# Ten accumulating DMA issues moved behind GpSimd's small operations, and one difference moved to the split that uses it

## The chip, the cores and the metric

The kernel runs on one core of a Trainium2 chip. Five engines work from queues of their own, each strictly in its program's order: TensorE (PE in the profile; its weight loads are PEld), VectorE (DVE), ScalarE (ACT), GpSimd (POOL) and SyncE (SP, which here only issues DMAs). They meet through semaphores alone. The metric is the device time of one execution in microseconds, the median of several runs.

## The reference

A transformer block on x of 2048 tokens by 448 channels, all in float32, with six modulation vectors from a small product of silu(c):

```python
h = layernorm(x) * (1 + ca) + sa
x = x + ga * A(h)          # linear attention, 16 heads of 28
h = layernorm(x) * (1 + cb) + sb
x = x + gb * B(h)          # token-mixing MLP
# B: h' = layernorm(h); u = gelu(h'^T w1 + b1); y = u w2 + b2, transposed back
```

A computes q, k, v, applies phi(t) = t + 1 or exp(t), sums phi(k)^T v over the tokens, divides phi(q) times that sum by phi(q) times the sum of phi(k), and multiplies by wo. B mixes tokens: its first product contracts 2048 tokens into 1792 features for every channel, its second one goes back to 2048. Note that there are two norms in a row before B: the block's own, with its modulation, and the one inside B.

## The kernel before, in words

Tokens go in 16 tiles of 128 (NT), features in 14 blocks of 128 (NF). Every large product is made from float32 operands that are split into a high and a low part: high is a rounded copy made on ScalarE, low is the difference, and three matmuls (high by high, high by low, low by high) give the sum. The low part is made in one of two ways. `split` (line 81) lets VectorE subtract. For ten pieces of w1 (`PIECE_DMA`, pieces 8 to 17) `split_to` (line 309) does without VectorE: ScalarE writes high (line 316) and then minus high into the low tile (line 317), and a DMA that GpSimd issues adds the full value onto it (line 318, `accum_op` add).

The order of all work is written out by hand; the order in which the program's lines run is the order on each engine's queue. Tiles come from pools of equal slots, and a slot's next owner waits until the last reader of the old one is done.

**First stage around the change: the loop at line 891**, laps i = 0 to 20. A lap holds several tokens tiles at different depths, so that each engine finds work:

- TensorE: four transposes of tile i (lines 779 and 780, written to `tq`), eleven matmuls of the output product of tile i - 1 (L804), in the first laps a projection of q, and from lap 5 on twelve matmuls of B's first product with token tile i - 5 (`step`, lines 854 to 856, `up`). From lap 17 on twelve more, of the second group of features. Without a projection that is 27 instructions a lap.
- ScalarE: the copies of the transposes (`pth`, lines 784 and 785), the second norm's output `y` (L845, needs `nb` and `rt`) and its high part `h2h` (L848), the two sums of squares `sqa` and `sqb` (L330), then the two halves of a w1 piece (`ph`, `pl`, lines 316 and 317).
- VectorE: residual, products, both steps of the first norm (lines 823 and 827), the reciprocal of `den` (L764), the scaled `pn` that the next lap's transposes read (L768), the low part `h2l` (L851). In laps 13 to 16 one step of the last modulation vector each (`mod_part`, lines 235 and 237).
- GpSimd: `nb` = mean by reciprocal root (L844), `nm` = minus mean (L818), `den` plus a small number (L761), `ny` = minus mean (L832), and at the lap's end the variance `vw` (L837) and the reciprocal roots `rt` of both norms (L839). `rt` of one lap is read by `nb`, `y` and the first norm of the next.

`split_to` is called at the lap's end (line 959), so the DMA issue of a piece stands on GpSimd behind `rt` and ahead of the next lap's `nb`. Piece k is made in lap k - 2; pieces 0 to 15 are used in lap k + 5, pieces 16 and 17 in laps 17 and 18.

**Second stage: B's second product** (from line 1193 on). It is done for pairs of token tiles q = 0 to 7, each with seven products m = 0 to 6 of sums and differences of four quadrants of w2 (a11, a12, a21, a22; Strassen's scheme in Winograd's form): s1 = a21 + a22, s2 = s1 - a11, s3 = a22 - s2, s4 = a12 - s2. The first sum is made by a DMA that adds a22 onto a21 in place (line 1024). The others are made by `sub` (line 1026) on VectorE, two instructions each (pieces of 512 and 384 columns, L1030), called from `split7` (line 1040) behind the split of the product whose row in `PRODS` (line 1035) names them: s2 behind m = 1, s3 behind m = 2, s4 behind m = 3. The splits run ahead of the products in the order `cuts` (line 1126): (q, m) = (0,0), (0,1), (0,3), (1,0), (1,1), (0,2), (1,3) and so on. The first five of them, thus s2 of the second pair too, are called in the last lap of the first product (`PRE2`, line 35), ahead of the gelu, the product with the modulation (L988) and the operand sums of the last two feature blocks (`finish_u`, line 982; `ub`, `ta`, `tb`, `ut`), which run as jobs at the start of the second product.

Of the kernel before, what the change touches and what calls it, by code (L numbers as in the profile page):

```python
# [11 lines left out]
ALU = mybir.AluOpType  # L12
# [38 lines left out]
def block_kernel(ctx: ExitStack, tc: tile.TileContext, x, xt, wqkv, wo, w1, b1, w2, b2, c, wmod, wfirst, out):  # L51
    nc = tc.nc
# [25 lines left out]
    def bank(name):  # L78
        return psum.tile([P, 512], F32, name=name, tag="bank")

    def split(full, hi, lo):
        nc.scalar.activation(hi, full, AF.Copy)  # L82
        nc.vector.tensor_sub(lo, full, hi.bitcast(F32))  # L83
# [51 lines left out]
    def load_mod(j):  # L135
        for k in range(4):
            wm[j, k] = (tslot if j == 5 else slot)(f"wm{j}_{k}", parts=G)
            nc.sync.dma_start(wm[j, k], wmod[k * G:(k + 1) * G, j * D:(j + 1) * D])
# [55 lines left out]
    def mod_out(j, ps):  # L194
        mods[j] = cst.tile([P, D], F32, name=f"mod{j}")
        nc.scalar.activation(mods[j], ps[:, :D], AF.Copy, bias=1.0 if j == 4 else 0.0)
# [35 lines left out]
    def mod_part(j, k):  # L232
        if k == 0:
            macc[j] = (tslot if j == 5 else slot)(f"acc{j}", parts=G)
            nc.vector.tensor_scalar_mul(macc[j], wm[j, 0], sc[:G, 4:5])
        else:
            nc.vector.scalar_tensor_tensor(macc[j], wm[j, k], sc[:G, 4 + k:5 + k], macc[j], op0=ALU.mult, op1=ALU.add)


    def mod_split(j):  # L240
        acc = macc.pop(j)
        macc[j] = (moving(slot, f"mh{j}", parts=G), moving(slot, f"ml{j}", parts=G))
        split(acc, *macc[j])

    def mod_sum2(j):
        ps = bank(f"modp{j}")
        hi, lo = macc.pop(j)
        nc.tensor.matmul(ps[:, :D], ones_r[:G, :], hi, start=True, stop=False)
        nc.tensor.matmul(ps[:, :D], ones_r[:G, :], lo, start=False, stop=True)
        return ps  # L250
# [49 lines left out]
    def load_to(i):  # L300
        while done["load"] < min(i, len(pieces)):
# [4 lines left out]
                              w1[t * P:(t + m) * P, f0 * P:(f0 + n) * P].rearrange("(t p) f -> p t f", p=P))  # L306
            done["load"] += 1

    def split_to(i):
        while done["split"] < min(i, len(pieces)):  # L310
            k = done["split"]
            new = tslot if k in TOKP else slot
            hi, lo = new(f"ph{k}", dt=F32R, w=512), new(f"pl{k}", dt=F32R, w=512)
            if k in PIECE_DMA:
                full = raws.pop(k)
                nc.scalar.activation(hi, full, AF.Copy)
                nc.scalar.activation(lo, hi.bitcast(F32), AF.Copy, scale=-1.0)
                nc.gpsimd.dma_start(lo, full, accum_op=ALU.add)  # L318
            else:
                split(raws.pop(k), hi, lo)  # L320
            parts[k] = (hi, lo)
            done["split"] += 1
# [5 lines left out]
    def b_square(src, nm, acc, name):  # L328
        dst = junk if name[0] == "s" else slot(f"sq{name}")
        nc.scalar.activation(dst, src, AF.Square, bias=nm, accum_out=acc)  # L330
# [127 lines left out]
    def a_q(t):  # L458
        project(t, 0, "qp")
        qps[t] = close(t, 0)  # L460
        del heads[t]

    def a_exp_q(keep=0):
        for t in sorted(qps)[:len(qps) - keep]:
            q_exp(qps.pop(t), t)
# [309 lines left out]
    def b_transpose(t):  # L775
        pn = pns.pop(t)
        tps[t] = bank(f"tq{t}")
        for ch in range(3):
            nc.tensor.transpose(tps[t][:, ch * P:(ch + 1) * P], pn[:, ch * P:(ch + 1) * P], ident)
        nc.tensor.transpose(tps[t][:64, 384:], pn[:, 384:D], ident)  # L780

    def b_high(t):
        phs[t] = (slot(f"pth{t}", 512, F32R), slot(f"ptl{t}", 384, F32R))
        nc.scalar.activation(phs[t][0][:, :384], tps[t][:, :384], AF.Copy)
        nc.scalar.activation(phs[t][0][:64, 384:], tps[t][:64, 384:], AF.Copy)
# [9 lines left out]
    def b_out(t):  # L795
        ph, pl = phs.pop(t)
        opb[t] = bank(f"op{t}")
        todo = []
        for ch in range(3):
            s = slice(ch * P, (ch + 1) * P)  # L800
            todo += [(ph[:, s], Wph[ch]), (ph[:, s], Wpl[ch]), (pl[:, s], Wph[ch])]
        todo += [(ph[:, 384:], Wph[3]), (ph[:, 384:], Wpl[3])]
        for n, (a, b) in enumerate(todo):
            nc.tensor.matmul(opb[t][:, :D], a, b, start=(n == 0), stop=(n == len(todo) - 1))  # L804

    def b_sums(i):
        if i not in vss:
            vss[i] = small.tile([P, 2], F32, name=f"vs{i}", tag="vs")
        return vss[i]
# [20 lines left out]
    def b_mean2(t, i):  # L830
        nm2s[t] = small.tile([P, 1], F32, name=f"ny{t}", tag="ny")
        nc.gpsimd.tensor_scalar_mul(nm2s[t], sums.pop(t), -1.0 / D)  # L832
        b_square(ys[t], nm2s[t], b_sums(i)[:, 1:2], f"b{t}")
# [24 lines left out]
    def step(f0, t, accs, mh, ml):  # L858
        k, at = place[f0, t]
        hi, lo = parts[k]  # L860
        for i, ps in enumerate(accs):
            acc3(ps, hi, lo, slice(at + i * P, at + (i + 1) * P), mh, ml, t == 0, t == NT - 1)
        if place.get((f0, t + 1), (0, 0))[0] != k:
            del parts[k]
# [26 lines left out]
    for i in range(NT + LAG):  # L891
        if i == NT - 4:
            load_mod(5)
        if NT - 3 <= i <= NT:
            mod_part(5, i - NT + 3)
        if i == NT:
            mod_split(5)
        if i < NT:
            b_transpose(i)
        if 0 <= i - 1 < NT:  # L900
            b_out(i - 1)
        nq = min(len(late), QS.get(i, 1))
        for _ in range(nq):
            a_q(late.pop(0))
        t = i - LAG
        if t >= 0:
            if t == 0:
                accs = [bank(f"up{f}") for f in range(4)]
            if i > NT:
                if not early:  # L910
                    early = [bank(f"up{W1G[1][0] + f}") for f in range(W1G[1][1])]
                r = i - NT - 1
                step(W1G[1][0], r, early, H2h[r], H2l[r])
            step(0, t, accs, H2h[t], H2l[t])
        if i == NT:
            mp = mod_sum2(5)
            mod_out(5, mp)
        if i < NT:
            b_high(i)
        a_exp_q(nq)  # L920
        scale, res, norm1, norm2 = i + 1 < NT, 0 <= i - 2 < NT, 0 <= i - 3 < NT, 0 <= i - 4 < NT
        if res and i < NT + 1:
            b_res(i - 2)
        if scale:
            b_prod(i + 1)
        if norm2:
            b_norm2(i - 4, i)
        if res:
            b_mean1(i - 2, i)
        if norm1:  # L930
            b_norm1_a(i - 3)
        if scale:
            b_sum(i + 1)
        if norm1:
            b_norm1_b(i - 3, i)
        if scale:
            b_eps(i + 1)
        if i < NT:
            b_low(i)
        if norm1:  # L940
            b_mean2(i - 3, i)
        if scale:
            b_recip(i + 1)
        if i < NT:
            b_low_last(i)
        if scale:
            b_scale(i + 1)
        if i == NT:
            b_res(i - 1)
        if norm2:  # L950
            b_low2(i - 4)
        if i == 0:
            for ch in range(4):
                wp_split(ch)
        a_phi_q(nq)
        load_to(max(14 + (i + 1) // 2, 12 + max(0, i - 6) + max(0, i - 14)))
        if res or norm1:
            b_rstd(i, 0 if res else 1, 2 if norm1 else 1)
        split_to(8 + max(0, i - 5))
# [66 lines left out]
    def sub(q, out, a, b, op=ALU.subtract, into=None):  # L1026
        res = []
        for i, (r0, n) in enumerate(RS):
            w = raw2[q, into][i] if into else slot(f"{out}_{q}_{r0}", n * P)
            nc.vector.tensor_tensor(w, raw2[q, a][i], raw2[q, b][i], op=op)  # L1030
            res.append(w)
        raw2[q, out] = res


    PRODS = (("a11", "b11", 0, None), ("a12", "b21", 1, ("s2", "s1", "a11")),
             ("s2", "t2", 0, ("s3", "a22", "s2", ALU.subtract, "a11")),
             ("s1", "t1", 2, ("s4", "a12", "s2", ALU.subtract, "a12")), ("s3", "t3", 0, None),
             ("s4", "b22", 2, None), ("a22", "t4", 0, None))

    def split7(q, m):  # L1040
        a, _, _, add = PRODS[m]
        hilo[q, m] = []
        for w, (r0, nr) in zip(raw2[q, a], RS):
            h, l = slot(f"{a}h_{q}_{r0}", nr * P, F32R), slot(f"{a}l_{q}_{r0}", nr * P, F32R)
            split(w, h, l)
            hilo[q, m].append((h, l))
        if add:
            sub(q, *add)

    def mult7(q, m, r0, r1):  # L1050
# [215 lines left out]
```

## Time and profile before

| | |
|---|---|
| three runs | 445.61, 445.74, 446.75 us; median 445.74 |
| the profiled execution | 445.55 us, of which 443.7 are its span (first to last instruction) |
| granted TensorE clock, mean | 0.997 |
| busy: TensorE, VectorE, ScalarE, GpSimd | 434.0, 363.9, 278.8, 112.2 us |
| DMA | 65.94 MB, of it 14.78 by the queue that GpSimd feeds |

In the profile's rows a name like L318 is a line of the kernel; `out<-in` are the tiles written and read, with buffer numbers left out. A timeline row has start and length in us, engine, line, operation, tiles, shape and count, and in brackets the idle time of the engine before it with what ended it. A chain row has start, length, engine, tile and line. A wait row names the waiting line, the one waited for, the sum, how often and the longest. A matmul's drawn length contains its way through the array, and the next one starts before it ends.

### The profile page before, as it was taken

The numbers are of one execution on the slowest core, as the hardware profiler recorded it, in microseconds if no ns is written. First come the engines' busy times: TensorE is split into PE (matmuls) and PEld (weight loads), VectorE is DVE, ScalarE is ACT, GpSimd is POOL, SyncE is SP. The second block draws the span as 40 slices with busy tenths as digits, with TensorE's granted clock in tenths as the row PEclk, the third lists the DMA queues.
The fourth block names the chain that finished last, engine by engine and source line by source line (L and its number), as shares of the span: only waits on it lengthen the run. The fifth ranks groups of instructions, "written<-read, shape, count | busy, mean of one in ns | idle before, by whom it ended". The sixth has DMA issues, their size and how long they took to land.

```text
span 443.7 us, 7292 instructions
## 1 busy us (share of the span) xinstructions
PE 434.0 (98%) x2376; PEld 399.7 (90%) x2376; DVE 363.9 (82%) x821; ACT 278.8 (63%) x598; POOL 112.2 (25%) x201
## 2 busy tenths in 40 slices
PE   8999999999999999999999999999999999999996
PEld 7878899999899998889999999999989999999995
DVE  4989997699799999996569785829599998898893
ACT  4899877748667777776774263627285555645550
POOL 3227554200025455554300000010101331132010
PEclk9999999999999999999999999999999999999998
DMA  7997999555400035334516661578269977986332
GB/s 251 386 308 161 214 236 221 106 162 172 127 5 1 24 72 139 78 71 95 190 55 189 215 189 45 148 209 226 46 189 206 204 173 169 224 173 123 60 41 41
DMA packets 63797, 65.94 MB, mean 149 GB/s; under 512 B 4944, under 2 KB 55312, under 8 KB 63760
## 3 DMA queue, kind: packets, MB, share of 16 engines
q1 hardware_dynamic: 54688, 50.71, 38.0%
q0 software_dynamic: 9072, 14.78, 20.8%
q8 instruction: 18, 0.29, 0.3%
q14 instruction: 19, 0.16, 0.1%
HBM read 45.88 MB, written 7.34 MB: 120 GB/s over the span
## 4 chain that ended last, share of the span: by engine, by line
PE 79%; ACT 10%; DMA 3%; DVE 3%; POOL 2%; issue 2%; SPq 0%; POOLq 0%; ACTq 0%; DVEq 0%
PE y L1062 16%; PE y L1063 8%; PE cacc L524 8%; PE up L856 8%; PE up L855 8%; PE up L854 8%; PE qp L420 7%; PE kp L420 6%; PE op L804 3%; POOL pl L318 2%; ACT y L845 1%; ACT sqa L330 1%; DMA a<-in_B_w_dram 1%; DMA a<-a 1%; ACT sqb L330 1%
## 5 line engine op out<-in xcount | busy, mean ns | idle before, releaser
L855 PE MATMUL up<-h2l,ph 128*128 128x448 f32 x224 | 81.3, 363 | 0.0
L856 PE MATMUL up<-h2h,pl 128*128 128x448 f32 x224 | 81.2, 362 | 0.0
L854 PE MATMUL up<-h2h,ph 128*128 128x448 f32 x224 | 80.8, 361 | 0.0
L1024 POOL DMA_DIRECT2D a<-a x16 | 14.2, 958 | 143.0 <-DVE u L988 75.2
L855 PEld LDWEIGHTS up<-h2l,ph 128*128 128x128 f32 x224 | 42.0, 188 | 3.4 <-DVE h2l L851 0.3
L854 PEld LDWEIGHTS up<-h2h,ph 128*128 128x128 f32 x224 | 41.9, 187 | 3.0
L856 PEld LDWEIGHTS up<-h2h,pl 128*128 128x128 f32 x224 | 42.0, 188 | 2.3
L83 DVE TENSOR_TENSOR pl<-pr,ph 128x512 fp32r<-128x512 f32 x46 | 30.8, 686 | 4.1 <-ACT ph L82 3.3
L82 ACT ACTIVATE ph<-pr 128x512 fp32r<-128x512 f32 x46 | 27.6, 623 | 0.8 <-PE up L856 0.5
L1068 ACT ACTIVATE cc<-y 128x448 f32<-128x448 f32 x24 | 12.9, 542 | 21.3 <-PE y L1063 21.3
L1082 POOL DMA_DIRECT2D out_dram<-yt x15 | 13.5, 903 | 48.0 <-DVE yt L1073 37.4
L988 DVE TENSOR_TENSOR u<-u,mod 128x448 f32<-128x448 f32 x14 | 8.7, 621 | 19.8 <-ACT u L987 19.6
L524 PE MATMUL cacc<-pkh,xh 128*128 128x448 f32 x64 | 24.4, 382 | 0.3 <-ACT pkh L498 0.3
L804 PE MATMUL op<-wph,pth 128*128 128x448 f32 x64 | 24.5, 383 | 0.0
L987 ACT ACTIVATE u<-up,b1c 128x448 f32<-128x448 f32 x14 | 8.8, 625 | 24.1 <-PE up L856 23.5
L420 PE MATMUL kp<-wh,hh 128*128 128x448 f32 x64 | 23.2, 372 | 0.6 <-ACT wh L256 0.6
L524 PE MATMUL cacc<-pkl,xh 128*128 128x448 f32 x64 | 23.3, 364 | 0.2 <-DVE pkl L500 0.2
L420 PE MATMUL qp<-wh,hh 128*128 128x448 f32 x64 | 23.3, 364 | 0.0
L804 PE MATMUL op<-wpl,pth 128*128 128x448 f32 x64 | 23.1, 362 | 0.0
L845 ACT ACTIVATE y<-y,nb,rt 128x448 f32<-128x448 f32 x16 | 12.2, 761 | 12.7 <-POOL nb L844 12.7
L1062 PE MATMUL y<-ut,s1h 128*128 128x448 f32 x56 | 18.2, 376 | 0.6 <-DVE ut L83 0.6
L1030 DVE TENSOR_TENSOR a<-a,s 128x512 f32<-128x512 f32 (+1 forms) x32 | 18.4, 617 | 0.0
(236 smaller groups left out, 1368.0 us busy)
## 6 DMA issues: line engine op xcount, KB each, us to landing
pr<-in_B_w_dram SPq DMA_DIRECT2D x56, 256.0 KB, 3.2
a<-in_B_w_dram SPq DMA_DIRECT2D x32, 256.0 KB, 4.8
a<-in_B_w_dram SPq DMA_DIRECT2D x32, 192.0 KB, 4.6
xt<-in_xt_dram SPq DMA_DIRECT2D x16, 256.0 KB, 4.9
x<-in_A_x_dram SPq DMA_DIRECT2D x16, 224.0 KB, 4.9
out_dram<-x SPq DMA_DIRECT2D x15, 224.0 KB, 2.2
out_dram<-yt POOLq DMA_DIRECT2D x15, 224.0 KB, 6.3
wm<-in_B_wmod_dram SPq DMA_DIRECT2D x16, 196.0 KB, 5.1
```

The lines of the kernel that those rows point to most:

```text
L82: nc.scalar.activation(hi, full, AF.Copy)
L83: nc.vector.tensor_sub(lo, full, hi.bitcast(F32))
L420: nc.tensor.matmul(pps[t, j][:, :D], a[:, ch * P:(ch + 1) * P], w, start=first, stop=False)
L524: nc.tensor.matmul(cacc[ch][:, :D], a[:, s], b, start=(t == 0 and i == 0), stop=(t == NT - 1 and i == len(todo) - 1))
L804: nc.tensor.matmul(opb[t][:, :D], a, b, start=(n == 0), stop=(n == len(todo) - 1))
L845: nc.scalar.activation(ys[t], ys[t], AF.Identity, bias=nb, scale=rs)
L854: nc.tensor.matmul(ps[:, :D], hi[:, sl], mh, start=first, stop=False)
L855: nc.tensor.matmul(ps[:, :D], hi[:, sl], ml, start=False, stop=False)
L856: nc.tensor.matmul(ps[:, :D], lo[:, sl], mh, start=False, stop=last)
L1030: nc.vector.tensor_tensor(w, raw2[q, a][i], raw2[q, b][i], op=op)
L1062: nc.tensor.matmul(ps[:, :D], h[:, s], w, start=opens and r == 0, stop=False, skip_group_check=True)
L1063: nc.tensor.matmul(ps[:, :HD], l[:, s], wh, start=False, stop=closes and r == PAIRS - 1, skip_group_check=True)
```

## The change

The ten DMA issues are no longer written where the piece's low part is begun. `split_to` puts them in a list, and the loop at line 891 empties the list in its next lap, behind `b_mean2`, that is behind `nb`, `nm`, `den` and `ny` on GpSimd and ahead of `vw` and `rt`. The rows of pieces and everything ScalarE does for them stay where they were.

For the second pair alone, s2 is no longer made behind the split of m = 1 but behind the split of m = 3 (which splits s1), directly ahead of s4, which reads it. For all other pairs the order stays.

```diff
+    low_dma = []
+
+    def split_end():
+        while low_dma:
+            nc.gpsimd.dma_start(*low_dma.pop(0), accum_op=ALU.add)
+
     def split_to(i):
...
                 nc.scalar.activation(lo, hi.bitcast(F32), AF.Copy, scale=-1.0)
-                nc.gpsimd.dma_start(lo, full, accum_op=ALU.add)
+                low_dma.append((lo, full))
...
         if norm1:
             b_mean2(i - 3, i)
+        split_end()
         if scale:
             b_recip(i + 1)
...
             hilo[q, m].append((h, l))
-        if add:
+        if (q, m) == (1, 3):
+            sub(q, *PRODS[1][3])
+        if add and (q, m) != (1, 1):
             sub(q, *add)
```

## The prediction

> **What bounds the kernel now.** I began with the page: the busy shares, then the chain of waits by line.
>
> ```profile
> span 443.7 us, 7292 instructions
> PE 434.0 (98%) x2376; PEld 399.7 (90%) x2376; DVE 363.9 (82%) x821; ACT 278.8 (63%) x598; POOL 112.2 (25%) x201
> PE y L1062 16%; PE y L1063 8%; PE cacc L524 8%; PE up L856 8%; PE up L855 8%; PE up L854 8%; PE qp L420 7%; PE kp L420 6%; PE op L804 3%; POOL pl L318 2%; ACT y L845 1%; ACT sqa L330 1%; DMA a<-in_B_w_dram 1%; DMA a<-a 1%; ACT sqb L330 1%
> ```
>
> TensorE is busy 98% and carries most of the chain, so only time in which it stands still can be won. Yet a GpSimd DMA issue (L318), which computes nothing, holds 2% of the chain. So I read TensorE's own waits next (time, times, longest).
>
> ```profile
> PE tq L779 <- DVE pn L768: 1.8, 6, 0.5
> PE y L1062 <- DVE ut L83: 0.6, 1, 0.6
> ```
>
> The other five rows of that answer lie in the first 34 us. The change touches both of these: L779 opens each lap of the loop at line 891, L1062 is the first product pass. The loss is larger than these rows say, since a matmul is drawn 0.36 us long while the next starts after 0.20. The timeline of TensorE gives the starts of L779 in laps 7, 9 and 15 (start, length):
>
> ```profile
> 155.31 0.49 PE L779 MATMUL tq<-ident,pn 128*128 128x128 f32 x3
> ...
> 165.42 0.49 PE L779 MATMUL tq<-ident,pn 128*128 128x128 f32 x3
> ...
> 198.62 0.52 PE L779 MATMUL tq<-ident,pn 128*128 128x128 f32 x3 [0.54 <-DVE pn L768]
> ```
>
> Where TensorE doesn't wait, a lap takes (165.42 - 155.31) / 2 = 5.055 us; the next six take 33.20 together. At its own pace they would take 30.33, so 2.87 us are lost there. What sets the longer lap is in the chain in order of time:
>
> ```profile
> 163.46 0.77 ACT y L845
> 164.25 0.58 ACT h2h L848
> 164.83 0.65 ACT sqa L330 x2
> 165.48 0.65 ACT sqb L330 x2
> 166.13 0.53 ACT ph L316
> 166.69 0.63 ACT pl L317
> 167.32 0.39 ACT pth L784
> 167.72 0.94 POOL pl L318
> 168.66 0.24 POOL nb L844
> ```
>
> It is a closed ring, 168.92 - 163.46 = 5.46 us long: ScalarE's y to pl, then the issue of pl's DMA on GpSimd, then the small nb behind it in GpSimd's order, then the next y. The issue stands between pl and an nb that needs nothing of it.
>
> **The change, part by part.** It adds and removes no instruction; it moves ten DMA issues (pl 8 to 17) on GpSimd and two subtractions on VectorE.
>
> *The issues.* In the built order each goes from the head of GpSimd's lap (ahead of nb, nm, den, ny) to behind ny, ahead of vw and rt. No other queue is passed; behind the issue wait vw and rt alone, and rt is what the next nb and the next norm need. One lap of GpSimd:
>
> ```profile
> 162.25 0.94 POOL L318 DMA_DIRECT2D pl<-pr  x1 [0.27 <-ACT pth L784]
> ...
> 164.06 0.22 POOL L832 TENSOR_SCALAR ny<-sy 128x1 f32<-128x1 f32 x1
> 166.21 0.19 POOL L837 TENSOR_SCALAR vw<-vs 128x2 f32<-128x2 f32 x1 [1.93 <-ACT sqb L330]
> 166.49 0.97 POOL L839 TENSOR_TENSOR rt<-vw,mhalf 128x2 f32<-128x2 f32 x1
> ```
>
> GpSimd idles 1.93 us between ny and vw, and the issue takes 0.94: it goes into the hole. Two rings are left. ScalarE alone: from y at 163.46 to the end of pth at 167.71 is 4.25 us. Through rt: sqb lets vw start at 166.21, rt ends at 167.46, nb takes 0.24 behind a gap of 0.08, the next y would start at 167.81: 4.35. Both are under TensorE's 5.055, so TensorE takes the lap over, if VectorE lets it. VectorE's rows:
>
> ```profile
> 158.54 0.25 DVE L764 RECIPROCAL den<-den 128x16 f32<-128x16 f32 x1 [0.23 <-POOL den L761]
> ...
> 164.01 0.25 DVE L764 RECIPROCAL den<-den 128x16 f32<-128x16 f32 x1 [0.42 <-POOL den L761]
> ...
> 164.62 0.62 DVE L768 SCALAR_TENSOR_TENSOR pn<-pq,den 128x448 f32<-128x448 f32 x1
> ...
> 187.59 0.45 DVE L235 TENSOR_SCALAR acc<-wm,sc 112x448 f32<-112x448 f32 x1
> ...
> 193.15 0.68 DVE L237 SCALAR_TENSOR_TENSOR acc<-wm,sc,acc 112x448 f32<-112x448 f32 x1
> ```
>
> It waits for den, which stands behind the issue, nb and nm; with the issue gone den is 0.9 us earlier and the 0.42 falls away. VectorE's own lap is then 5.46 - 0.42 = 5.04, level with TensorE's. Is it ahead? The pn for the L779 of 165.42 ended at 165.24; without the two waits at 164.59. Six laps later, with the modulation rows of 0.45 and 0.68 in between and the 0.15 from pn's end to a waiting L779, it allows 164.59 + 30.24 + 1.13 + 0.15 = 196.11. TensorE's own pace gives 165.42 + 30.33 = 195.75. So the L779 of 198.62 comes between 195.75 and 196.15, and the gain is 2.5 to 2.9. I take 2.7: it is close between the engines, and the waits' true length is nearer 0.5 (VectorE's instructions overlap by some hundredths).
>
> The issue in its new place isn't in the trace. By the rows it costs from 0.92 (the shortest of its own) to 1.48 (the longest of its kind, L507):
>
> ```profile
> L318 POOL DMA_DIRECT2D pl<-pr x10: 920/937/965, 156.7 to 206.4; - x10
> ...
> DMA to landing us min/median/max: 3.3/3.4/6.3
> ...
> L507 POOL DMA_DIRECT2D pk<-pk x11: 877/1216/1484, 34.5 to 83.6; - x11
> ```
>
> If ScalarE starts sqb the moment ny is there, vw may start 0.85 behind ny's end (sqb 0.65, its readout and the step 0.2). An issue of length I, started 0.07 behind ny, then holds vw for I - 0.78: 0.16 us at 0.94, 0.70 at 1.48. The ring through rt grows from 4.35 to 4.51, or to 5.05, and still isn't the longest. So the move costs 0 at both ends of the rows. I take 0.94, its own median in the same loop.
>
> pl also lands later: the issue moves 164.28 + 0.07 - 162.25 = 2.1 us down the lap. Pieces 8 to 15 are used five or more laps later. The last, pl 17, is the tight one; its issue goes behind the ny of lap 16, and its first use is in the second row:
>
> ```profile
> 209.18 0.21 POOL L832 TENSOR_SCALAR ny<-sy 128x1 f32<-128x1 f32 x1 [0.79 <-DVE y L827]
> ...
> 214.15 0.36 PE L856 MATMUL up<-h2h,pl 128*128 128x448 f32 x1
> ```
>
> From 209.46 with 3.4 to the landing it is there at 212.9, 1.3 before its use; with the worst landing, 6.3, TensorE would stand 1.6 us, once. I take 0, by the median. The loads that reuse pr's buffers follow the landings, on SP's queue, but bring pieces 22 and on, which are used several steps behind piece 17.
>
> *The subtractions.* The second pair's s2 = s1 - a11 (L1030, two instructions) now stands on VectorE behind the split of s1 and ahead of s4 = a12 - s2. VectorE, TensorE and ScalarE before:
>
> ```profile
> 315.35 0.69 DVE L1030 TENSOR_TENSOR s<-a,a 128x512 f32<-128x512 f32 x1 [2.37 <-issue]
> 318.04 0.56 DVE L1030 TENSOR_TENSOR s<-a,a 128x384 f32<-128x384 f32 x1 [1.99 <-DMA a<-a]
> 318.51 0.62 DVE L988 TENSOR_TENSOR u<-u,mod 128x448 f32<-128x448 f32 x1
> ...
> 324.24 1.15 DVE L1030 TENSOR_TENSOR a<-a,s 128x512 f32<-128x512 f32 x2
> ...
> 325.14 0.27 PE L1063 MATMUL y<-ub,a12l 128*128 128x224 f32 x1
> 326.05 0.47 PE L1062 MATMUL y<-ut,s1h 128*128 128x448 f32 x1 [0.64 <-DVE ut L83]
> ...
> 330.86 0.38 PE L1062 MATMUL y<-ut,s3h 128*128 128x448 f32 x1
> 331.32 0.37 PE L1063 MATMUL y<-ut,s3l 128*128 128x224 f32 x1
> ...
> 314.15 0.64 ACT L987 ACTIVATE u<-up,b1c 128x448 f32<-128x448 f32 x1 [3.36 <-PE up L856]
> ```
>
> Both subtractions wait for an accumulating DMA, and everything VectorE still owes to the last pair of u is queued behind them. That u is ready at 314.79, but its product starts at 318.51: 3.7 us. From it hangs the ut for which TensorE waits at 326.05. Moved up by 3.7 it ends near 322.3, 2.9 before its use. In their new place the two cost what the x2 row of 324.24 costs, 1.1 us, ahead of s3l, which TensorE met at 331.32: -3.7 + 1.1 puts it 2.6 earlier, also in time. So TensorE's gaps close: 326.05 - 325.14 less the usual step 0.10 is 0.81; the slow step behind it 0.10; 331.32 - 330.86 less 0.21 is 0.25. Sum 1.16, the upper bound; the lower is 0, if the stall only changes its name. I take 1.16, as both margins are twice the gaps. Behind the first stage's gain all this comes 2.7 earlier; should the DMA not follow, it is now awaited by the s1 split, used at 328.7, with room.
>
> *The sum.* 2.7 + 1.16 = 3.86. The profiled execution took 445.55 (1.85 around its span): 441.7. The median shown, 445.74, lies 0.19 higher, which is inside this sum's error.
>
> **The rivals.** *VectorE binds the loop.* Its lap is as long as TensorE's, and GpSimd's issue now runs beside other VectorE work. At 5.2 a lap the L779 of 198.62 comes at 164.59 + 31.2 + 1.28 = 197.1, the gain is 1.5, and the time 445.55 - 2.7 = 442.9. For it: 5.04 against 5.055. Against: every VectorE length above already has GpSimd working beside it.
>
> *The second part pays nothing.* The 1.1 us in the new place, or ScalarE's splits behind it, make s3l or ut late again: 445.55 - 2.7 = 442.9. For it: s3l was late already, and the pair goes in ahead of it. Against: 4.4 us of VectorE's idle time (2.37 and 1.99) end.
>
> *Slower: the issue holds vw.* In the new place it runs beside VectorE's two-input operations (pn, h2l), and rt behind it closes the ring. If the issue had to sit out two such operations of 0.62, I = 2.2, vw is held 1.4, the lap is 5.75, and nine laps lose 9 x 0.29 = 2.6 against before; less 1.16 that is 447.0, and 452 with three. It decides above I = 1.9, where the lap is 5.46 again. Against: ten issues at 0.92 to 0.965 in a loop where VectorE is never idle for that long, and none of the eleven of L507 above 1.48. The Trainium skill ("SBUF — State Buffer", sections "SBUF: two separate sides" and "A bandwidth-pool intuition that's wrong (but worth ruling out)") speaks for this rival: GpSimd and VectorE share a port pair under an exclusive lock, and a GpSimd-issued DMA of about 620 ns takes about 3100 beside a VectorE copy. By its 3.1 the lap would be an estimated 6.67 and the time 455; the 0.94 of this loop disagrees.
>
> *It does nothing.* If the ring were closed by pth (the releaser that the profile names for the issue) and not by the issue, y would start no earlier: 444.4 with the second part's gain alone, 445.6 without it.
>
> **How the numbers follow.** Forecast 0.64, VectorE binds 0.12, second part nothing 0.12, slower 0.07, nothing 0.05. A difference under 0.3% (1.3 us) can't be told from none here; the first three lie beyond it: faster 0.88, same 0.05, slower 0.07. The range starts 0.7 under the forecast (the loop's full 2.9 is 0.2 of it, the scatter of the three runs below their median 0.13; the rest is left for what I have not seen) and ends at 443.6, which takes in both partial cases and half of one late landing: 441.0 to 443.6.
>
> **What would show it.** Right: L779 starts 5.05 apart through lap 15 and near 195.9 there; GpSimd's issue stands in the former idle time before vw, still about 0.94; ScalarE no longer waits for nb; L988 follows the last gelu at once; the waits for pn and ut are gone from TensorE's list. Wrong: issues over 1.5 us, vw waiting on the issue, L779 still 5.4 apart, a wait for pl near lap 18, or for s3l near 327.

## The result and the profile after

| | before | changed |
|---|---|---|
| median of six runs each, side by side | 445.94 us (445.61 to 447.34) | 442.79 us (441.48 to 443.62) |
| the profiled execution | 445.55 us | 442.58 us |
| its span | 443.7 us | 440.9 us |

The ratio is 0.992, 95% interval 0.9898 to 0.9942: a gain of 2.6 to 4.5 us. The forecast was 441.7.

The page of the changed kernel, its span, busy shares and the chain of waits by engine:

```profile
span 440.9 us, 7297 instructions
...
PE 432.9 (98%) x2376; PEld 400.8 (91%) x2376; DVE 363.2 (82%) x821; ACT 278.7 (63%) x598; POOL 119.2 (27%) x201
...
PE 94%; DVE 2%; ACT 1%; DMA 1%; SPq 0%; issue 0%; ACTq 0%
```

GpSimd's DMA issue and ScalarE's ring have left the chain; 94% of it is TensorE. TensorE's whole list of waits has five rows, all from the first 35 us:

```profile
PE warm L181 <- DVE roots L104: 1.1, 1, 1.1
PE rw L399 <- DVE rowst L391: 0.3, 1, 0.3
PE cacc L530 <- ACT pkh L504: 0.2, 1, 0.2
PE kp L426 <- ACT wh L256: 0.2, 1, 0.2
PE cacc L530 <- DVE pkl L506: 0.2, 1, 0.2
```

The waits for `pn` and `ut` are gone. In TensorE's timeline the first transpose of laps 6 and 15 (L785, L779 before) and the last matmul of the kernel:

```profile
150.32 0.49 PE L785 MATMUL tq<-ident,pn 128*128 128x128 f32 x3
...
195.80 0.38 PE L785 MATMUL tq<-ident,pn 128*128 128x128 f32 x2
...
434.93 0.26 PE L1072 MATMUL y<-ut,a22l 128*128 128x224 f32 x1
```

Nine laps take 195.80 - 150.32 = 45.48, that is 5.053 each. The same two ends before:

```profile
150.26 0.49 PE L779 MATMUL tq<-ident,pn 128*128 128x128 f32 x3
...
439.04 0.26 PE L1063 MATMUL y<-ut,a22l 128*128 128x224 f32 x1
```

From the first transpose of lap 6 to the last matmul it was 439.04 - 150.26 = 288.78 us, and is 434.93 - 150.32 = 284.61 now: 4.17 less. This stretch will be the yardstick below, because it leaves out how a run starts and how it ends. The span fell by 2.81 only. The missing 1.36 is 0.06 at the start and 1.30 at the end: from the last matmul to the end of the span it was 4.65 before and is 5.95 now. TensorE is done by then; two stores are in flight. The view of the plain store by line (tile 15's, two halves; the last to be issued is the max) gives their landing before, and then after:

```profile
DMA to landing us min/median/max: 1.7/2.1/2.5
```

```profile
DMA to landing us min/median/max: 1.7/2.7/3.6
```

The accumulating store of tile 14, issued by GpSimd 1.6 us ahead of that last half (434.49 in the changed kernel), landed after 4.95 us, against 3.63 before. So the loop gave all that was forecast and more, and the end of this one execution gave 1.3 back. Whether the change does that is the main thing to settle.

GpSimd in one lap of the changed kernel, and VectorE beside its `den`:

```profile
168.45 0.94 POOL L313 DMA_DIRECT2D pl<-pr  x1 [0.24 <-issue]
169.47 0.50 POOL L843 TENSOR_SCALAR vw<-vs 128x2 f32<-128x2 f32 x1
170.05 0.72 POOL L845 TENSOR_TENSOR rt<-vw,mhalf 128x2 f32<-128x2 f32 x1
170.85 0.20 POOL L850 TENSOR_TENSOR nb<-ny,rt 128x1 f32<-128x1 f32 x1
171.02 0.66 POOL L824 TENSOR_SCALAR nm<-sm 128x1 f32<-128x1 f32 x1
172.21 0.64 POOL L767 TENSOR_SCALAR den<-den 128x16 f32<-128x16 f32 x1 [0.52 <-DVE den L764]
```

```profile
171.51 0.61 DVE L764 TENSOR_REDUCE den<-pd 128x16 f32<-128x448 f32 x1
172.04 0.67 DVE L833 SCALAR_TENSOR_TENSOR y<-y,rt,mod 128x448 f32<-128x448 f32 x1
```

The issue fills the former hole and `nb` follows `rt` at once. It is GpSimd now that waits for VectorE's reduction (L764), not VectorE for `den`.

### The profile page after: what moved, and what is told of

It is laid out like the page before. It is cut to its first block, busy times and chain, and to the rows that moved or that the text cites. A ratio compares the mean times of both kernels' runs of the same rounds, so it can differ in the third digit from the quotient of the medians.

```text
span 440.9 us, 7297 instructions
## 1 busy us (share of the span) xinstructions
PE 432.9 (98%) x2376; PEld 400.8 (91%) x2376; DVE 363.2 (82%) x821; ACT 278.7 (63%) x598; POOL 119.2 (27%) x201
## 4 chain that ended last, share of the span: by engine, by line
PE 94%; DVE 2%; ACT 1%; DMA 1%; SPq 0%; issue 0%; ACTq 0%
PE y L1071 19%; PE up L860 10%; PE up L861 10%; PE up L862 10%; PE y L1072 9%; PE op L810 8%; PE cacc L530 8%; PE qp L426 7%; PE kp L426 6%; PE tq L785 1%; DMA xt<-in_xt_dram 1%; PE qp L433 1%; PE kvb L741 1%; PE rowb L283 1%; PE wp L877 1%; PE kp L433 1%
## 5 line engine op out<-in xcount | busy, mean ns | idle before, releaser
L995 DVE TENSOR_TENSOR u<-u,mod 128x448 f32<-128x448 f32 x14 | 8.7, 621 | 21.7 <-ACT u L994 21.5
L767 POOL TENSOR_SCALAR den<-den 128x16 f32<-128x16 f32 x16 | 8.8, 548 | 47.3 <-DVE den L764 47.3
L348 POOL TENSOR_TENSOR mv<-ve,roots 128x2 f32<-128x2 f32 (+1 forms) x13 | 12.8, 983 | 21.2 <-DVE ve L377 17.8
```

## The experiments

Every kernel was run beside the kernel before on its chip. "Stretch" is, as above, from the first L785 (or L779) at 150 to 151 us to the last matmul; "end" is from there to the end of the span; the last column is when the store issued last but one (tile 14's, on GpSimd unless it is plain) landed, counted from its issue.

| kernel | median us | ratio, 95% interval | stretch | end | landing |
|---|---|---|---|---|---|
| before | 445.94 | | 288.78 | 4.65 | 3.63 |
| changed | 442.79 | 0.992, 0.9898 to 0.9942 | 284.61 | 5.95 | 4.95 |
| e1 issues alone | 443.24 | 0.9927, 0.991 to 0.9944 | 285.99 | 4.82 | 3.79 |
| e2 subtraction alone | 445.65 | 0.9979, 0.9967 to 0.999 | 287.51 | 6.36 | 5.35 |
| e3 two issues each | 442.46 | 0.9904, 0.9889 to 0.9919 | 284.96 | 4.75 | 3.84 |
| e4 changed | 443.27 | 0.992, 0.9907 to 0.9933 | 284.61 | 6.38 | 5.38 |
| e5 issue behind nb | 443.38 | 0.9934, 0.992 to 0.9948 | 285.53 | 4.97 | 3.97 |
| e6 changed, plain store | 441.43 | 0.9888, 0.9873 to 0.9902 | 284.61 | 4.99 | plain |
| e7 four issues each | 453.23 | 1.0153, 1.0139 to 1.0168 | 295.16 | 6.05 | 5.17 |
| e8 changed, plain store | 441.08 | 0.9892, 0.9867 to 0.9916 | 284.61 | 4.69 | plain |
| e9 before, plain store | 445.46 | 0.9988, 0.9974 to 1.0003 | 288.28 | 5.08 | plain |
| e10 changed | 442.43 | 0.9922, 0.9897 to 0.9946 | 284.61 | 4.81 | 3.81 |

The medians of before were 446.73 beside e1 to e4, 446.12 beside e5 to e7, 445.79 beside e8 to e10.

### The two parts apart: e1, e2, e4

e1 is the changed kernel with s2 of the second pair back behind m = 1; e2 is the kernel before with only that subtraction moved; e4 is the changed kernel again. e1's edit against the changed kernel:

```diff
-        if (q, m) == (1, 3):
-            sub(q, *PRODS[1][3])
-        if add and (q, m) != (1, 1):
+        if add:
             sub(q, *add)
```

> The ten DMA issues stand behind ny as in the changed kernel; the second pair's s2 stays behind the split of m = 1. If the two parts are independent, TensorE's loop laps are 5.05 us through lap 15 and its waits for ut (0.8 us) and s3l (0.25) are back: the last matmul starts 2.8 to 2.9 us earlier than in the kernel before (at 436.2), and the time is 2.8 under it. If the second part was what paid, the last matmul moves by less than 1.5. Should the tail behind the last matmul (4.4 us in the kernel before, 5.7 in the changed one) be longer because of the moved issues, it is 5.7 here; if it varies by chance from execution to execution, it can be anything from 4.4 to 5.9.

> Only the second pair's s2 is moved; the issues stand ahead of nb as before. If the parts are independent: loop laps of 5.46 as before, no wait for ut or s3l, the last matmul 1.1 to 1.25 us earlier than in the kernel before, the time 1.1 to 1.2 under it. If the first part's gain is what makes the second one possible, the last matmul moves by less than 0.5. Tail by the theory that this part lengthens it: 5.7; by chance: 4.4 to 5.9.

> The changed kernel once more, for its tail. Its last matmul stood 4.1 us earlier than before, but its span was only 2.8 shorter. If the tail (last matmul to end of span) varies by chance with the landing of the last two stores, this execution has the last matmul at 434.9 again and a tail that can be anywhere between 4.4 and 5.9 us, and the times spread by about 2 us as before, with the fastest at 441.5. If the change makes the tail longer, it is 5.7 again.

TensorE's waits behind 150 us, first in e1, then in e2:

```profile
PE y L1069 <- DVE ut L83: 0.8, 1, 0.8
```

```profile
PE tq L779 <- DVE pn L768: 1.8, 6, 0.5
```

Each part takes away its own wait and leaves the other's. In the stretch the issues are worth 288.78 - 285.99 = 2.79 and the subtraction 1.27; together 4.06, of the 4.17. (e1's last matmul stands at 437.04 and not at the expected 436.2, because that execution reached lap 6 later, by 0.79.) The 0.11 between lies behind the loop. From the first transpose of lap 6 to that of lap 15 it is 48.36 before and 45.48 both in e1 and in the changed kernel: 2.88 less. Behind that, e1 waits 0.8 for `ut` where the kernel before waits 0.6. That the shorter loop makes this wait longer isn't shown, for in e9 below, whose loop is that of before, it is 0.2:

```profile
PE y L1062 <- DVE ut L83: 0.2, 1, 0.2
```

In all three VectorE waits for the DMA that adds a22 onto a21: 1.99 us before, 1.76 in e9, 2.10 in e1. So the second part takes away a wait whose length changes from one execution to the next. From lap 15 to the last matmul it is 240.42 before, 239.94 in e9 and 240.51 in e1, against 239.13 in the changed kernel and 239.15 in e2: this part is worth 0.8 to 1.4, and 1.27 is its worth against one execution of before.

In e4 the stretch is 284.61 again, to the hundredth, and so it is in e6, e8 and e10: what scattered between these executions of the changed kernel lay ahead of 150 us or behind the last matmul. For the kernel before the stretch did move, by 0.50 (e9). e4's times lay 0.84 apart, where some 2 was expected, and its end, like e2's, is longer than any that was expected.

### The place of the issue, and its length: e3, e5, e7

e3 doubles the suspected cost, e7 makes it four times as many; the bytes stay the same.

```diff
-                low_dma.append((lo, full))
+                low_dma.extend((lo[:, c:c + 256], full[:, c:c + 256]) for c in (0, 256))
```

In e7 the step is 128, four times. e5 calls `split_end()` behind `nb` already, ahead of `nm`, `den` and `ny`:

```diff
         if scale:
             b_prod(i + 1)
         if norm2:
             b_norm2(i - 4, i)
+        split_end()
...
-        split_end()
```

> The changed kernel, but each of the ten accumulating DMAs is issued as two of 256 columns, so that GpSimd spends 1.9 us on issues behind ny instead of 0.94. By the prediction's ring through rt the issue time costs nothing up to about 1.5 us and reaches the old lap at 1.9: with 1.9 the laps are 5.4 to 5.5 again, vw waits for the issue and not for sqb, ScalarE waits for nb again, the first part's gain of 2.9 us is gone, and the last matmul starts 1.1 to 1.5 us earlier than before. If GpSimd's place in the lap were free whatever stands there, the laps stay at 5.05 and the last matmul keeps its 4.1 us.

> The changed kernel, with each of the ten accumulating DMAs issued as four of 128 columns, some 3.7 us of issues in a lap. Theory (the issues share GpSimd's queue with vw, rt, nb, nm, den and ny; two of them, 1.87, filled it to 5.2 a lap, and TensorE's lead hid that): lap about 7.0, ScalarE waits 2 us or more for nb, TensorE waits for pn in each of laps 9 to 17, L785 of 195.80 comes 14 us or more later, time 455 to 460. Rival (the place behind ny is free whatever is put there, because nothing that sets the lap waits behind it): laps under 5.4, time under 446.

> The changed kernel, with the issue one place up: behind nb alone, still ahead of nm, den and ny. Theory (only nb closes the ring, nm and den have room): L785 stays 5.05 apart from lap 7 to 15, TensorE has no waits for pn, the gaps of TensorE's starts stay near 1.7 us in sum, last matmul within 0.3 of 434.9, time that of the changed kernel, 442.8 within 0.7. Rival (the den behind the issue was VectorE's wait and half of the gain): den comes 0.6 to 0.9 later than in the changed kernel, VectorE waits for it ahead of the reciprocal, its lap grows from 4.94 to 5.3 or more, L785 of 195.80 comes at 197.5 to 199, time 444 to 445.

e3, which should have been slower, lost nothing that its median shows, and 0.35 of the stretch. The timeline of one of its laps, and TensorE's first transpose of lap 15:

```profile
168.37 0.22 POOL L838 TENSOR_SCALAR ny<-sy 128x1 f32<-128x1 f32 x1
...
168.60 0.65 ACT L336 ACTIVATE sqa<-x,nm 128x448 f32<-128x448 f32 x1
...
168.84 1.87 POOL L313 DMA_DIRECT2D pl<-pr  x2 [0.24 <-ACT h2h L854]
...
169.26 0.66 ACT L336 ACTIVATE sqb<-y,ny 128x448 f32<-128x448 f32 x1
...
169.82 0.19 ACT L336 ACTIVATION_READ_ACCUMULATOR sqb<-y,ny 128x1 f32 x1
...
170.78 0.65 POOL L843 TENSOR_SCALAR vw<-vs 128x2 f32<-128x2 f32 x1
...
179.04 1.86 POOL L313 DMA_DIRECT2D pl<-pr  x2 [0.27 <-ACT h2h L854]
...
196.21 0.52 PE L785 MATMUL tq<-ident,pn 128*128 128x128 f32 x3 [0.17 <-DVE pn L774]
```

The issues do cost twice, 1.87. But `sqb` begins 0.67 behind the end of `ny`, since ScalarE is still at `sqa`; its readout ends at 170.01 and the issues at 170.71, so `vw` is held 0.70, not the 1.09 that the formula I - 0.78 gives. ScalarE now waits for `nb`, 5.3 us in eight laps, yet TensorE meets a late `pn` once, by 0.32 us (196.21 - 150.41 = 45.80 for nine laps, against 45.48). From 168.84 to 179.04 two laps of GpSimd take 10.20, that is 5.10 each, a little over TensorE's 5.055: the lead of the engines ahead of TensorE paid for the difference until lap 15.

e7 is where the cover ends. From GpSimd's timeline two laps' blocks of issues and three of the six operations between them, and ScalarE's only wait in 156 to 212 us:

```profile
179.53 3.63 POOL L313 DMA_DIRECT2D pl<-pr  x4
183.23 0.19 POOL L843 TENSOR_SCALAR vw<-vs 128x2 f32<-128x2 f32 x1
183.50 0.72 POOL L845 TENSOR_TENSOR rt<-vw,mhalf 128x2 f32<-128x2 f32 x1
...
185.12 0.27 POOL L767 TENSOR_SCALAR den<-den 128x16 f32<-128x16 f32 x1
...
185.65 3.64 POOL L313 DMA_DIRECT2D pl<-pr  x4
```

```profile
ACT y L851 <- POOL nb L850: 16.7, 8, 4.0
```

GpSimd works without a break from the one block to the next: 185.65 - 179.53 = 6.12 a lap, of which 3.63 are issues and 2.49 everything else. It has become the engine that sets the lap. The stretch is 10.55 longer than the changed kernel's and the time 453.23: far slower, as the theory said, but not the 455 to 460 that I expected, because I had added e3's longer `vw` and `rt` (0.65 and 1.04), which here take 0.19 and 0.72. One lap of 8.36 us has a hole of 2.25 on GpSimd ahead of its fourth issue that the profile puts down to nothing; its cause stays open. From 2.49 + I an estimate of the price at which the lap of before, 5.46, is reached again is 3.0 us of issues; the prediction had 1.9. Where the issues begin to cost can't be taken from this sum: it would say 2.6, for 5.055, but e3's lap of 5.10 with 1.87 is already past that point, because GpSimd's other operations take longer there. So it lies near 1.9.

e5 fell between its two theories. Its timeline, VectorE in the first lap with a moved issue, two later laps of GpSimd and TensorE's lap 15, and ScalarE's wait in 156 to 200 us:

```profile
159.51 0.25 DVE L770 RECIPROCAL den<-den 128x16 f32<-128x16 f32 x1 [0.78 <-POOL den L767]
...
167.83 0.94 POOL L313 DMA_DIRECT2D pl<-pr  x1 [0.39 <-issue]
168.52 0.67 POOL L824 TENSOR_SCALAR nm<-sm 128x1 f32<-128x1 f32 x1
...
172.86 0.92 POOL L313 DMA_DIRECT2D pl<-pr  x1 [0.39 <-issue]
...
197.06 0.41 PE L785 MATMUL tq<-ident,pn 128*128 128x128 f32 x2 [0.38 <-DVE pn L774]
```

```profile
ACT sqa L336 <- POOL nm L824: 3.0, 8, 0.4
```

The lap is 172.86 - 167.83 = 5.03: with the issue ahead of `nm`, ScalarE's `sqa` waits 0.4 a lap for `nm`, and a ring through `nm`, `sqa`, `sqb`, `vw`, `rt` and `nb` closes just under TensorE's 5.055. That is enough for the plain laps. But VectorE loses 0.78 in the first of them, where `den` stands behind the issue, and then, tied to 5.03 instead of its own 4.94, gathers next to no lead; when the modulation rows come in laps 13 to 16, `pn` is late, by 0.90 in lap 15 (197.06 - 150.68 = 46.38, against 45.48). So the rival's wait for `den` did come, once, and its longer laps did not. The stretch is 0.92 longer: two thirds of the first part's 2.79 come from freeing `nb`, one third from putting the issue behind `nm`, `den` and `ny` as well.

### The end of the span: e6, e8, e9, e10

In e6 and e8 tile 14 is stored as tile 15 is: its x is parked in DRAM (not in SBUF, as e6's expectation has it) and fetched back near the end, VectorE adds to it, and SP stores two plain halves, in place of the last accumulating store. e9 is the same edit on the kernel before, e10 the changed kernel again.

```diff
         elif m == 5:
             out2(q, 2, "c2", t0, 1)
-            add_to_x(t0)
+            if q == NS7 - 1:
+                finish(t0, HD, yt(t0)[:, HD:])
+            else:
+                add_to_x(t0)
...
-    xpark = {t: park.tile([P, D], F32, name=f"xpark{t}") for t in range(NT - 1, NT)}
+    xpark = {t: park.tile([P, D], F32, name=f"xpark{t}") for t in range(NT - 2, NT)}
...
+            fetch_x(NT - 2)
```

The other half is finished in the same way behind m = 1.

> The changed kernel, with tile 14 stored as tile 15 is: its x parked in SBUF, added on VectorE and stored plainly in two halves by SP, in place of the last accumulating store from GpSimd. Theory (the time from the last matmul to the span's end is set by the landing of that accumulating store, 3.6 to 3.8 us or 5.0 to 5.4, and of the plain store queued behind it): last matmul unchanged near 434.9, the span ends 3.9 to 4.7 behind it, not 4.65 to 6.4; median 441.0 to 441.9, lowest and highest run less than 1.2 us apart. Rival (the scatter is of the end of any program, not of that store): tail still 4.7 to 6.4, median near 442.8, runs as far apart as before.

> The changed kernel with tile 14 stored plainly, once more, beside the two next ones on one chip. Theory (the accumulating store of tile 14 sometimes lands late, 5 us and more, and then holds up the plain store behind it by 1.2 to 1.5 us; without it that can't happen): last store lands within 2.7 us of its issue, the span ends 4.6 to 5.0 behind the last matmul, median 441.0 to 441.9, runs within 1.2 us. Rival (the tight runs of the first time were chance): runs 1.5 us and more apart, median over 442.3.

> The kernel before with tile 14 stored plainly, and no part of the change. Theory (the late landing has nothing to do with the change, and the loop's gain nothing with the store): last matmul near 439.0, as before, the span ends 4.6 to 5.0 behind it, median 445.0 to 445.7, runs within 1.2 us; against the changed kernel with the same store the difference is 3.9, the whole predicted sum, within 0.5. Rival (the change itself makes the end longer): the plain store gains under 0.3 here, and the difference between the two plain kernels is over 4.5.

> The changed kernel again, beside the two with the plain store. Theory: last matmul near 434.9; the accumulating store lands either 3.6 to 4.0 or 4.9 to 5.4 us behind its issue, and the span ends 4.6 to 5.0 or 5.9 to 6.4 behind the last matmul, by which of the two it is; median 442.5 to 443.3, runs 1.3 us or more apart. Rival (the end of the span is scattered evenly, by no one transfer): a landing between these two, or a tail that doesn't go with it.

The same view by line of the plain stores: in e8 (four halves), then in e4 and in e10 (the two halves of tile 15); the max is the last store:

```profile
DMA to landing us min/median/max: 1.6/1.7/2.2
```

```profile
DMA to landing us min/median/max: 1.7/2.9/4.1
```

```profile
DMA to landing us min/median/max: 1.7/2.1/2.5
```

e4 and e10 are one kernel with one stretch, and their ends differ by 1.57: in e4 the accumulating store landed after 5.38 and the plain one behind it after 4.1, in e10 after 3.81 and 2.5. Over the nine executions in the table that end with an accumulating store its landing took 3.63 to 3.97 five times and 4.95 to 5.38 four times, never between, and the end is about one us longer than the landing each time. The late landing isn't the change's doing: e2, whose loop is that of before, has it, and e10 hasn't. What one profile of each kernel can't tell is whether it is as frequent in both; that stays open.

In the three executions with the plain store it didn't occur: their last store landed after 2.5, 2.2 and 2.6. The end was 4.99 and 4.69, the medians 441.43 and 441.08, against 442.79, 443.27 and 442.43 of the changed kernel; the interval of e6 (0.9873 to 0.9902) ends below that of e4 (from 0.9907). The medians of this version lie below those of both kernels, though e8's interval overlaps that of e10, which ran beside it. Its ends are no shorter, though, than the short ones with the accumulating store (4.65 to 4.97): what is won is that the long ones are gone, and four long of nine would make less of a difference on average than the 1.35 us between the medians of e8 and e10, so the profiles may show too few long ones, or something else helps. Expectations missed as well: e6's end was to lie under 4.7, the runs of e9 were up to 2.1 us apart where 1.2 was expected, so other things scatter too; e8's, 1.23 apart, and e10's median, 442.43, fell just outside what was expected. e9 is not a clean test either: its median is 0.33 under that of before, with an interval that includes no gain; the wait for `ut` shrank in its profile, from 0.6 to 0.2, which accounts for the 0.50 of stretch, while its end (5.08) is no shorter. Between e9 and e8 lie 4.38 us of median, which fits the sum of 3.86 and the stretch's 4.17 alike.

## Why the prediction was right, point by point

*What bounds the kernel: right.* The ring of 5.46 with the issue in it was what made the lap longer. e1 shows it: the issues alone out of it, and L785 comes 5.05 apart.

*The first part: 2.7 forecast, 2.79 measured (2.88 in the laps alone), inside 2.5 to 2.9.* It came out near the upper bound because VectorE's lap was mis-sized: 5.04 forecast, level with TensorE's, 4.94 measured, from the two rows of one instruction a lap apart:

```profile
160.50 0.62 DVE L760 SCALAR_TENSOR_TENSOR pd<-pq,zb 128x448 f32<-128x448 f32 x1
...
165.44 0.62 DVE L760 SCALAR_TENSOR_TENSOR pd<-pq,zb 128x448 f32<-128x448 f32 x1
```

The wait for `den` was taken as the 0.42 that the row before shows; 5.46 - 4.94 is 0.52, near the 0.5 that the text named as its true length and didn't subtract. So VectorE gains 0.11 on TensorE in each lap and has lead when the modulation rows come. L785 came at 195.80 (195.75 to 196.15 forecast). The rival in which VectorE binds is out here; e5 shows how near it was, since there 0.78 at the start and laps of 5.03 make `pn` late. The rival in which the change does nothing is out by e1.

*The issue in its new place costs nothing: right, with a wrong formula.* It takes 0.92 to 0.965 as before:

```profile
L313 POOL DMA_DIRECT2D pl<-pr x10: 920/936/965, 158.7 to 205.0; - x10
...
DMA to landing us min/median/max: 3.3/3.8/5.5
```

The assumption "If ScalarE starts sqb the moment ny is there" is the step that failed: ScalarE is still at `sqa`. At 0.94 that changes little: in the lap shown `vw` starts right behind the issue and 0.15 behind the end of `sqb`'s readout (169.32), where a hold of 0.16 was forecast. At 1.87 the formula was 0.39 too dear and made e3's expectation wrong. The Trainium skill ("SBUF — State Buffer", "A bandwidth-pool intuition that's wrong (but worth ruling out)") has 620 ns become 3100 beside a VectorE copy; that is the time of a DMA, which the prediction took for the length of an issue. The ten issues here did not grow at all: nine ran beside `pn` or `h2l`, and the last (0.93 at 205.02) with no VectorE instruction beside it. So the rival in which the issue holds `vw` for a microsecond or more didn't come; e3 and e7 show that its mechanism is real from some 1.9 us of issues on, where 1.87 cost 0.35 of the stretch and 3.63 cost 10.55. The same page, under "Who interferes with whom", says that a two-tensor VectorE instruction takes the shared pair's read side alone while descriptors need its write side, which it marks as inferred; the 0.92 to 0.965 agree with that.

*pl 17's landing, taken as 0: right.* No wait for `pl` appears; the longest landing of the ten was 5.5, under the 6.3 of before, and its issue came at 205.02, earlier than the 209.46 that was assumed.

*The second part: 1.16 forecast as the upper bound, 1.27 measured alone (e2).* The mechanism is right and the bound was passed. That the size came so near is in part luck: it was read from the execution that it is measured against, and against e9's it would be 0.8. The rows of VectorE and TensorE in the changed kernel:

```profile
311.96 0.62 DVE L995 TENSOR_TENSOR u<-u,mod 128x448 f32<-128x448 f32 x1 [1.83 <-ACT u L994]
...
318.76 0.69 DVE L83 TENSOR_TENSOR ut<-ta,ut 128x224 fp32r<-128x224 f32 x2
...
322.40 0.38 PE L1071 MATMUL y<-ut,s1h 128*128 128x448 f32 x1
...
325.10 1.15 DVE L83 TENSOR_TENSOR s3l<-a,s3h 128x512 fp32r<-128x512 f32 x2
...
327.32 0.26 PE L1072 MATMUL y<-ut,s3l 128*128 128x224 f32 x1
```

The product with the modulation (L995) now follows the gelu that it waited 3.7 us behind, `ut` ends at 319.45, 2.95 before its use (2.9 forecast), and s3l's second half at 326.25, ahead of 327.32. The rival in which this part pays nothing is out.

*The time: 441.7 forecast, 442.79 measured, and in the profiled execution 442.58.* The 0.88 between 441.7 and 442.58 adds up as follows, to within 0.02: the stretch fell by 0.31 more than the sum, the start was 0.06 later and the end 1.30 longer, while 0.15 less lay around the span (1.70 against 1.85). So the term that the sum had wrong is one that it didn't have: the end. The sum was set against an execution of before with a short end, 445.55, below all four medians of that kernel (445.79 to 446.73), and took the 0.19 between it and the first median for the whole scatter. Set against 446.0 the same sum gives 442.1. The measured ratios leave it there: 1 - 3.86/445.94 is 0.9913, inside each of the three intervals of the changed kernel.

## What to carry to other kernels

A DMA issue is an instruction on its engine's queue like any other: put it behind the operations that close a ring between engines, and then look at each small operation it still stands ahead of, since `nm`, `den` and `ny` together were worth a third of the first part's gain. Before a sum is set against one profiled execution, split that execution into the stretch that the change touches, its start and its end: here the changed kernel's stretch repeated to 0.01 us while its end jumped by 1.3 and more. A plain store at the end is worth trying: it took 1.35 off the median of the changed kernel, but off that of before only 0.33, which is not clear of noise.

## What was not expected of the hardware

*A landing with two lengths.* The same 224 KB accumulating store into DRAM, at the same place of the program, landed after 3.6 to 4.0 us or after 5.0 to 5.4 us, and the plain store of 112 KB behind it on another queue was late with it (2.5 to 2.7 or 3.6 to 4.1). Why there are two was not tried.

*GpSimd's small operations change their length with their neighbours.* `den`, 128 by 16 elements, takes 0.64 or 0.65 in each of the eight laps of the changed kernel from 157 to 194 us (the row at 172.21 is one). It begins there while VectorE's L833 (172.04 to 172.71) reads two tensors in SBUF, and ends 0.14 behind it. It takes 0.28 before, at 163.71, where no VectorE instruction runs beside it, and 0.27 in e7 (the row at 185.12), where VectorE's neighbour reads one of its two inputs from PSUM. All over GpSimd is busy 119.2 us instead of 112.2 with the same 201 instructions. The Trainium skill ("SBUF — State Buffer", "SBUF: two separate sides") says that a VectorE instruction with two SBUF inputs and a GpSimd operation that reads SBUF shut each other out for the whole of one of them; these rows agree.
